# Summing the exponentials of a batch element's head pairs on GpSimd instead of TensorE

## Chip, cores and metric

One NeuronCore of a Trainium2 chip runs the whole program. The metric is the device time of one execution in microseconds (us); lower is better. TensorE multiplies matrices (PE in the profile; its weight loads are PEld), VectorE is DVE, ScalarE is ACT, GpSimd is POOL, and SyncE (SP) issues most transfers.

## What is computed

Attention with normalised queries and keys, then an MLP mixer on its output. Eight batch elements, 12 heads of 64, 448 positions; d_model is 768. Cut to what matters here:

```python
q_n, k_n = rmsnorm(q, g_q), rmsnorm(k, g_k)
scores = q_n @ k_n.T / 8
attn = exp(scores - max);  attn /= attn.sum(-1)      # the sum is what the change moves
x = (attn @ v)                                       # (B, S, 768)
h = relu(x.T @ w_tok1) @ w_tok2;  u = x + h.T        # token mixing
out = u + relu(u @ w_ch1) @ w_ch2                    # channel mixing
```

q, k and v are float32. The four weights arrive as 64-bit floats, and the kernel converts them itself.

## The kernel before

The work goes by head **pairs** p (two heads side by side on 128 partitions, six pairs in an element) and by **two pairs** t (pairs 2t and 2t+1). The first element therefore has t = 0, 1, 2. There are two arms, chosen at run time by the size of g_q and g_k; with these inputs the arm without a subtracted maximum runs (`shifted` is false).

For each t there are seven key blocks k of 64 keys. `score(t, k)` makes two PSUM tiles of scores (pool `ps_S`, four buffers) and ScalarE turns them into one SBUF tile `e` of 128x896 exponentials (pool `e_pool`, four buffers). `values(ps, k)` multiplies them by V into `o_ps`. The sums over keys, the denominators, are made in one of two ways, by `on_pe(p)`:

- on TensorE: `values` also calls `ones`, which multiplies every `e` by a block of ones and accumulates over the seven k in a PSUM tile of the pool `ps_M`;
- by additions: `group_sums(t, k)` adds the seven tiles `e` into one tile `es` (pool `es_pool`, one buffer), six additions of 128x896 for each t, and `row_sums(t)` then multiplies `es` alone by the ones, into two tiles `d_ps` of `ps_S`.

Before the change the first element (p below 6) uses the first way and all others the second, with the additions on VectorE. An `e` tile is free again when `values` has used it and, in the second way, `group_sums` as well (`used`).

`att_step(g)` lists one quarter of a t in program order: scores, transposes of later queries and keys (`turn_qk`), values, then the other engines' pieces. Every engine executes its own instructions in the order in which they are issued. The pieces that matter besides:

- `pre.roots(n, st)` forms 1/rms of pairs n and n+1: `guess` on VectorE (line 1473), then for n = 4 to 10 three Newton steps of four small GpSimd instructions each (lines 1481 to 1484); `scale` multiplies queries and keys by it on VectorE (line 1502), and `turn_qk` transposes them on TensorE (line 430). roots(4) stand at the end of t = 0, scale(4) and scale(5) at the start of t = 1, their transposes at its end; the same for 6 and 7 in t = 1 and t = 2.
- `denominators` turns the sums into reciprocals and multiplies the outputs, on VectorE (lines 558, 560, 572, 575); ScalarE first copies `o_ps` to `uT` (line 566).
- `trans_x(0, j)` transposes pair j's result (lines 816 and 818) for the token mixing `tok1` (line 840).
- `weight_items` converts the weights, spread over the same stage: five VectorE instructions for each chunk of 128x512 (lines 346, 347, 349, 351 and 380) and one on ScalarE between the last two (line 357). Up to t = 2 all chunks are merged with the attention's items in proportion to their costs by `merge`, so that a list with more cost in it shifts them a little.

Of the kernel before, what the change touches and what calls it, by code (L numbers as in the profile page):

```python
# [13 lines left out]
ALU = mybir.AluOpType  # L14
# [69 lines left out]
def whole(ctx, tc, shifted, pre, q, k, v, g_q, g_k, moe_w_tok1, moe_w_tok2, moe_w_ch1, moe_w_ch2, out):  # L84


    nc = tc.nc
# [10 lines left out]
    NPAIR = H // 2  # L98
# [53 lines left out]
    st = dict(pre.st)  # L152
# [339 lines left out]
    def group_sums(t, k):  # L492

        if k == 1:
            st["es", t] = es_pool.tile([P, 2, S], F32, name="es")
        es = st["es", t]
        nc.vector.tensor_tensor(out=es[:], in0=(es if k > 1 else st["e", t, 0])[:], in1=st["e", t, k][:], op=ALU.add)  # L497
        for i in (0, 1) if k == 1 else (k,):
            used(t, i)

    def on_pe(p):

        return shifted or p < NPAIR

    def ones(p, moving, **kw):

# [5 lines left out]
    def used(t, k):  # L512

        n = st["uses", t, k] = st.get(("uses", t, k), 0) + 1
        if n == 1 + (not on_pe(2 * t)):
            st.pop(("e", t, k))

    def values(ps, k):

        kw = dict(start=(k == 0), stop=(k == NK - 1))  # L520
        for p in ps:
            if k == 0:
                st["o", p] = ps_O.tile([P, 512], F32, name="o_ps")
                if on_pe(p):
                    st["d", p] = s_tile("d_ps") if shifted else m_tile()
            e, vt = exps(p, k), st["v", p]
            for a in range(2):
                rows = rows_of(p, a)
                nc.tensor.matmul(  # L529
                    out=st["o", p][a * D:(a + 1) * D, 0:S], lhsT=vt[rows, k * D:(k + 1) * D], rhs=e[rows, :], **kw)  # L530
        for p in ps:
            if on_pe(p):
                ones(p, exps(p, k), **kw)
        if not shifted:
            used(ps[0] // 2, k)
# [49 lines left out]
    def big_step(t, second):  # L585
# [31 lines left out]
        if not second:  # L617
            squares = [item(fn, i, st) for i in (n, n + 1) for fn in (pre.square, pre.reduce)] if more else []
            ahead, beside = (squares[:1], squares[3:]) if t > BIG else ([], [])
            between = [item(group_sums, t, k) for k in (1, 2) if live]  # L620
            ends, roots = ([(0.4, fn) for fn in fns] for fns in (denominators(last), pre.roots(n, st) if more else []))
            if t == BIG:
                return ahead, (5.4, first_block), beside, between + ends + [
                    item(load_v, i, c=0.0) for i in pair] + squares + roots
            between += roots[:1] + ends[:2] + roots[1:2]
            between += [it for both in zip(ends[2:], roots[2:4]) for it in both] if more else ends[2:]
            between += roots[4:] + [item(load_v, i, c=0.0) for i in pair if live]
            return ahead, (5.4, first_block), beside, between
        beside = [item(scale, n), item(scale, n + 1), item(turn_qk, n, 1), item(turn_qk, n, 0)] if more else []
        beside += [item(group_sums, t, k) for k in (3, 4)]  # L630
        between = [item(turn_qk, n + 1, 1), item(turn_qk, n + 1, 0)] + loads(n + 2) if more else []
        between += [item(group_sums, t, k) for k in (5, 6)] + loads(n + 3)
        return [], (6.2, second_block), beside, between

# [611 lines left out]
    for b in range(B):  # L1246
# [35 lines left out]
        elif b + AHEAD < B:  # L1282
            t = (b + AHEAD) * NPAIR // 2
# [290 lines left out]
```

## Time and profile before

| what | value |
|---|---|
| median of 3 executions | 1281.13 us (1280.3 to 1282.95) |
| the profiled execution | 1280.59 us |
| its span, first to last instruction | 1278.8 us |
| TensorE busy | 1249.1 us (98%) |
| VectorE busy | 796.8 us (62%) |
| ScalarE busy | 393.6 us (31%) |
| GpSimd busy | 394.8 us (31%) |
| granted TensorE clock | 0.997 |

The profiled execution is 0.5 us below the median, and 1.8 us of it lie outside the span. Busy shares are means over the whole span. The stage that the change touches lies between 20 and 90 us from the start, and the views below are of that stretch.

A row of the profile gives the line, the engine, the operation, what it writes and reads, the shape and how often; then busy time, and the idle time before it with what ended it. A row of the timeline starts with the start time and the duration in us. One float32 matmul of the program appears as two records.

### The profile page before, as it was taken

How to read it: one execution, taken by the hardware profiler on the slowest of the kernel's cores; microseconds unless marked ns; L12 is line 12 of the kernel's file. 1: busy time of each engine (PE TensorE's matmuls, PEld its weight loads, DVE VectorE, ACT ScalarE, POOL GpSimd, SP SyncE). 2: the span in 40 equal slices, each digit the busy share in tenths (PEclk: the TensorE clock that was granted, in tenths of full speed). 3: DMA queues.
4: the chain of work that ended last, by engine and by line, in shares of the span. 5: the costliest groups of instructions: out<-in, count | busy, mean ns of one | idle time of the engine just before them, and what ended most of it. 6: DMA issues, size and time to landing. Idle time of an engine off the chain costs nothing.

```text
span 1278.8 us, 20023 instructions
## 1 busy us (share of the span) xinstructions
PE 1249.1 (98%) x7236; PEld 887.4 (69%) x7236; DVE 796.8 (62%) x1241; ACT 393.6 (31%) x785; POOL 394.8 (31%) x637
## 2 busy tenths in 40 slices
PE   5999999999999899999999999999999999999998
PEld 2444444457745487796778768885887867797998
DVE  6999869756663355855668356765558456554233
ACT  6663433124330144402433044311343024300210
POOL 2302552043995611331223112241122322131222
PEclk9999999999999899999999999999999999999999
DMA  8767486999789876695657767585766865386554
GB/s 204 172 179 200 144 228 167 217 260 253 212 220 236 188 171 162 140 258 112 161 151 178 190 143 187 139 220 120 188 158 146 234 130 144 114 207 142 191 173 105
DMA packets 486784, 228.37 MB, mean 179 GB/s; under 512 B 368276, under 2 KB 446996, under 8 KB 486676
## 3 DMA queue, kind: packets, MB, share of 16 engines
q1 hardware_dynamic: 479682, 213.33, 67.5%
q0 software_dynamic: 3968, 12.98, 3.3%
q8 instruction: 59, 0.97, 0.3%
q10 hardware_dynamic: 3026, 0.69, 0.3%
q14 instruction: 49, 0.40, 0.1%
HBM read 184.26 MB, written 42.66 MB: 177 GB/s over the span
## 4 chain that ended last, share of the span: by engine, by line
PE 88%; DVE 5%; DMA 2%; SPq 1%; ACT 1%; issue 1%; DVEq 0%; ACTq 0%
PE m_ps L1002 25%; PE m_ps L1068 22%; PE s_ps L456 9%; PE o_ps L529 9%; PE m_ps L882 6%; PE m_ps L972 5%; PE m_ps L1051 4%; PE m_ps L840 2%; PE t_ps L840 2%; PE d_ps L509 1%; PE m_ps L509 1%; DVE es L497 1%; DVE raw L349 1%; DVE raw L347 1%; PE t_ps L430 1%
## 5 line engine op out<-in xcount | busy, mean ns | idle before, releaser
L1068 PE MATMUL m_ps<-hb,unit 128*128 128x224 f32 x1440 | 277.2, 354 | 0.0
L1068 PEld LDWEIGHTS m_ps<-hb,unit 128*128 128x128 f32 x1440 | 271.0, 190 | 8.9 <-issue 7.7
L1002 PE MATMUL m_ps<-tu,unit 128*128 128x224 f32 x1008 | 201.6, 355 | 1.3 <-ACT r L1012 1.3
L1002 PEld LDWEIGHTS m_ps<-tu,unit 128*128 128x128 f32 x1008 | 189.1, 190 | 15.0 <-issue 9.2
L460 ACT ACTIVATE e<-s_ps 128x448 f32<-128x448 f32 x294 | 138.7, 553 | 178.4 <-PE s_ps L456 169.8
L1002 PE MATMUL m_ps<-uT,unit 128*128 128x224 f32 x756 | 151.1, 354 | 0.0
L1002 PEld LDWEIGHTS m_ps<-uT,unit 128*128 128x128 f32 x756 | 142.2, 190 | 6.9 <-issue 3.9
L456 PE MATMUL s_ps<-qkT 64*64 64x448 f32 x1260 | 143.7, 545 | 0.8 <-ACT x L822 0.8
L529 PE MATMUL o_ps<-e,v 64*64 64x448 f32 x1148 | 129.4, 538 | 0.3 <-ACT uT L566 0.2
L497 DVE TENSOR_TENSOR es<-es,e 128x896 f32<-128x896 f32 x90 | 101.8, 1131 | 13.3 <-ACT e L460 8.6
L1008 DVE TENSOR_TENSOR hb<-m_ps,r 128x448 f32<-128x448 f32 x63 | 39.2, 622 | 108.8 <-POOL r L1008 56.7
L1008 POOL TENSOR_TENSOR hb<-r,r 128x448 f32<-128x448 f32 x21 | 23.8, 1132 | 246.0 <-ACT r L1024 246.0
L456 PEld LDWEIGHTS s_ps<-qkT 64*64 64x64 f32 x1260 | 44.9, 132 | 70.1 <-issue 60.6
L529 PEld LDWEIGHTS o_ps<-e,v 64*64 64x64 f32 x1148 | 45.1, 133 | 63.9 <-issue 60.4
L1481 POOL TENSOR_TENSOR nt<-rs 128x56 f32<-128x56 f32 (+1 forms) x54 | 22.4, 415 | 196.4 <-DVE rs L1473 193.6
L1009 ACT ACTIVATE hb<-hb 128x448 f32<-128x448 f32 x84 | 48.4, 577 | 99.4 <-DVE hb L1008 77.7
L321 POOL TENSOR_TENSOR raw<-raw 128x128 f32<-128x128 f32 x128 | 65.1, 528 | 34.6 <-DMA raw<-wp 30.1
L1083 POOL TENSOR_TENSOR uT<-uT,r 128x448 f32<-128x448 f32 x42 | 51.4, 1238 | 78.5 <-DVE r L1083 46.7
L882 PE MATMUL m_ps<-w_sb,h 128*128 128x448 f32 x192 | 75.2, 544 | 0.0
L1451 DVE TENSOR_REDUCE ms<-sq 128x28 f32<-128x896 f32 (+2 forms) x44 | 47.4, 1079 | 36.3 <-ACT sq L1438 28.2
L1008 DVE TENSOR_TENSOR r<-m_ps,r 128x448 f32<-128x448 f32 x42 | 26.1, 622 | 64.5 <-PE m_ps L1002 64.5
L887 DVE TENSOR_TENSOR uT<-uT,m_ps 128x448 f32<-128x448 f32 x48 | 29.4, 614 | 59.1 <-PE m_ps L882 59.0
(148 smaller groups left out, 1607.8 us busy)
## 6 DMA issues: line engine op xcount, KB each, us to landing
unit<-ws SPq DMA_DIRECT2D x267, 384.0 KB, 4.1
raw<-in_moe_w_ch_dram SPq DMA_DIRECT2D x72, 256.0 KB, 3.5
v<-in_v_dram SPq DMA_DIRECT2D x96, 112.0 KB, 4.1
out_dram<-turned SPq DMA_DIRECT2D x182, 56.0 KB, 1.9
xs<-xt SPq DMA_DIRECT2D x56, 168.0 KB, 4.6
qk_t<-in_q_dram SPq DMA_DIRECT2D x144, 56.0 KB, 3.6
qk_t<-in_k_dram SPq DMA_DIRECT2D x144, 56.0 KB, 3.7
x<-xs SPq DMA_DIRECT2D x42, 192.0 KB, 3.7
```

What stands on the lines that cost most here:

```text
L321: nc.gpsimd.tensor_tensor(out=at[o], in0=at[x], in1=at[y], op=ALU.add if op == "+" else ALU.subtract)
L456: nc.tensor.matmul(out=pss[i][rows_of(i, a), 0:S], lhsT=qkT[h, 1, k * D:(k + 1) * D], rhs=qkT[h, 0, :], start=True, stop=True)
L460: nc.scalar.activation(out=e[:, i, :], in_=pss[i][:, 0:S], func=AF.Exp)
L497: nc.vector.tensor_tensor(out=es[:], in0=(es if k > 1 else st["e", t, 0])[:], in1=st["e", t, k][:], op=ALU.add)
L529: nc.tensor.matmul(out=st["o", p][a * D:(a + 1) * D, 0:S], lhsT=vt[rows, k * D:(k + 1) * D], rhs=e[rows, :], **kw)
L840: nc.tensor.matmul(out=st["t1", h][jc][:, 0:HC], lhsT=w1_sb[:, c, jc * P:(jc + 1) * P], rhs=st["x", b, h][:, :, c, :], start=start and c = ...
L882: nc.tensor.matmul(out=ps[:, 0:S], lhsT=st["h1", jc][:, cc * P:(cc + 1) * P], rhs=w2_sb[:, jc].rearrange("p c r -> p (c r)"), start=(jc == ...
L972: nc.tensor.matmul(out=ps, lhsT=a[:, o + 2 * half, :], rhs=natural(half * KF + t) if wide else u[:, half * KC + t, :], start=(t == 0 and h ...
L1002: nc.tensor.matmul(out=ps[:, j * HS:(j + 1) * HS], lhsT=w[:, t, j, :], rhs=m, start=(t == 0), stop=(t == KC - 1))
L1008: add = lambda e, o, x, y: e.tensor_tensor(out=o, in0=x, in1=y, op=ALU.add)
L1068: nc.tensor.matmul(out=ps[:, x * HS:(x + 1) * HS], lhsT=st["w"][:, tile_at % 6, :], rhs=hb[:, X_SLOT[f], i, :], start=(i == 0), stop=(i == 3))
L1083: e.tensor_tensor(out=get(out), in0=get(x_), in1=get(y), op=ALU.add if op == "+" else ALU.subtract)
```

## The change

For pairs 2 to 5 (t = 1 and t = 2 of the first element) the denominators are made by `group_sums` and `row_sums` instead of `ones`, and these additions are given to GpSimd. Pairs 0 and 1 stay on TensorE, and all later elements keep VectorE.

```diff
         es = st["es", t]
-        nc.vector.tensor_tensor(out=es[:], in0=(es if k > 1 else st["e", t, 0])[:], in1=st["e", t, k][:], op=ALU.add)
+        e = nc.gpsimd if 2 * t < NPAIR else nc.vector
+        e.tensor_tensor(out=es[:], in0=(es if k > 1 else st["e", t, 0])[:], in1=st["e", t, k][:], op=ALU.add)
         for i in (0, 1) if k == 1 else (k,):
             used(t, i)
 
     def on_pe(p):
 
-        return shifted or p < NPAIR
+        return shifted or p < 2
```

Through `on_pe`, three other places follow: `values` no longer calls `ones` for these pairs, `used` waits for two users of an `e` tile instead of one, and `att_step` adds the six `group_sums` items (cost 0.5 each in `merge`) and one `row_sums` for each t. The added line moves every later line number by one.

## The prediction

> **What bounds the kernel now.** I read the page first (TensorE busy 98% of the span), then the busy time by stretches over the stage concerned:
>
> ```profile
> 20.00:40.00 20.00, 19.93 (x198) 8.35 (x192) 18.08 (x34) 13.67 (x27) 2.87 (x5) 1.00 1.11 231
> 40.00:60.00 20.00, 19.76 (x186) 9.07 (x184) 19.31 (x34) 13.99 (x29) 4.74 (x12) 1.00 0.51 144
> 60.00:80.00 20.00, 19.27 (x180) 8.82 (x176) 18.91 (x34) 12.39 (x27) 4.27 (x8) 1.00 0.71 205
> ```
>
> The columns after the length are PE, PEld, DVE, ACT, POOL. TensorE sets the pace, but VectorE has only 0.7 to 1.9 us of 20 free; GpSimd is nearly empty. So TensorE time is worth something here only while VectorE keeps up. TensorE's timeline prices the removed matmuls:
>
> ```profile
> 53.05 0.93 PE L509 MATMUL m_ps<-e,one_c 64*64 64x448 f32 x8
> 53.80 0.93 PE L529 MATMUL o_ps<-e,v 64*64 64x448 f32 x8
> 54.56 0.93 PE L509 MATMUL m_ps<-e,one_c 64*64 64x448 f32 x8
> ```
>
> Start to start, one key block of ones for two pairs takes 0.75 us, as much as its values. Last, the timelines of VectorE, GpSimd and TensorE show who feeds whom between t = 1 and t = 2:
>
> ```profile
> 56.62 0.18 DVE L1473 TENSOR_SCALAR rs<-ms 112x32 int32<-112x32 int32 x1
> 56.88 0.95 POOL L1481 TENSOR_TENSOR nt<-rs 112x32 f32<-112x32 f32 x1 [14.39 <-DVE rs L1473]
> 67.20 2.35 DVE L1502 TENSOR_TENSOR qk_t<-qk_t,rs 112x1024 f32<-112x1024 f32 x2
> 70.34 1.91 PE L430 MATMUL t_ps<-ident,qk_t 112*128 112x112 f32 x16 [0.26 <-ACT e L460]
> ```
>
> VectorE's guess for pairs 6 and 7 starts GpSimd's twelve Newton steps (to 64.84), these release VectorE's scale (ends 69.55), and TensorE's transposes start 0.8 us later. The chain VectorE-GpSimd-VectorE-TensorE has under 1 us of slack, and the added work stands on its two middle engines.
>
> **What the skill says.** The Trainium skill, "SBUF — State Buffer", Who interferes with whom: VectorE and GpSimd share a pair of SBUF ports under an exclusive lock; a VectorE instruction with two SBUF inputs, or in a two-port mode, blocks and is blocked by a GpSimd instruction that reads SBUF. The trace agrees, to the instruction:
>
> ```profile
> 214.71 2.78 POOL L984 TENSOR_TENSOR uT<-uT,r 128x448 f32<-128x448 f32 x2 [18.00 <-ACT r L983]
> ...
> 214.51 0.69 DVE L349 SCALAR_TENSOR_TENSOR raw<-raw 128x512 uint32<-128x512 uint32 x1
> 215.24 1.25 DVE L351 TENSOR_SCALAR raw<-raw 128x512 uint32<-128x512 uint32 x1
> 216.41 3.15 DVE L497 TENSOR_TENSOR es<-es,e 128x896 f32<-128x896 f32 x2
> ```
>
> Line 351 takes 0.43 us elsewhere and 1.25 here; the first of the two line 497 additions takes 2.02 instead of 1.09. They alternate: one VectorE instruction, one of GpSimd. "GPSIMD Engine Reference", Elementwise: GpSimd needs 1.96 times VectorE's time for a float32 addition. The exact shape stands in the trace, at 1.92 times:
>
> ```profile
> L1042 DVE TENSOR_TENSOR hb<-hb x42: 1026/1082/2026, 494.0 to 1244.7; 128x896 f32<-128x896 f32 x42
> L1042 POOL TENSOR_TENSOR hb<-hb x18: 2074/2082/2092, 491.8 to 1254.9; 128x896 f32<-128x896 f32 x18
> ```
>
> **The change part by part.**
>
> Removed from TensorE: 7 blocks of ones for each t, 14 x 0.75 = 10.5 us; added: `row_sums` twice, 2 x 0.75 = 1.5. Net -9.0 us of TensorE work: the most that can be gained.
>
> Added to GpSimd: 12 x 2.08 = 25.0 us. In its queue six additions of t = 1 stand after Newton(4), then Newton(6), then the six of t = 2. With the lock, a blocked VectorE instruction loses about 1.93 of each 2.08 us (at 216.41 line 497 lost 0.93 behind the last 0.99 us of a GpSimd addition; start-up overlaps). Contended are lines 346, 347, 349, 351, 380, 497, 575, 1502; transposes, reductions and reciprocals run beside GpSimd (at 511 us line 558 keeps its 0.59).
>
> *t = 1.* ScalarE's exponential of k = 1 ends at 42.4 (41.47 plus two of 0.5), and Newton(4) by 42.5, so the first addition starts at 42.4. Each takes 2.08 plus about 0.5 waiting for VectorE's current instruction: 42.4 + 6 x 2.57 = 57.8. TensorE without its ones would reach `row_sums(1)` at 57.67 - 5.25 = 52.4; it waits until 57.8, adds 0.85 with the handover, and starts the next transposes at 58.7 instead of 57.67: **+1.0 us**, the gain of t = 1 gone. Behind that wait nothing else is lost. The earlier wait for scale(5), about 51 instead of 48.8, lies inside it.
>
> *VectorE's lag.* Six blocks of 1.93 are 11.6 us, 0.6 of it under one transpose: 11.0. The guess at 56.62 moves to about 68.0 (0.4 for handovers). Newton(6), 8.0 us before (56.88 to 64.84), takes 7.5: 68.2 to 75.7. Only then do the additions of t = 2 start.
>
> *t = 2.* By 76.2 VectorE has redone the work up to line 347 of the chunk before the scales. Left are lines 349 (0.55 after a release), 351 (0.3), a transpose (covered), 575 (0.5) and two 1502 (1.1 each), each preceded by one addition of 2.0: the scales end at 76.2 + 5 x 2.0 + 3.5 = 89.7, the sixth addition at 91.7. The transposes, held in TensorE's queue with all values and scores behind them, end at 90.7 instead of 72.2: +18.5. Four blocks without ones win back 3.0, `row_sums(2)` costs 0.75: the transposes at 79.11 come at 95.4, **+16.3**.
>
> *The end of the stage.* VectorE, free at 91.7, needs the 15.6 us of work that stood between 69.55 and 86.45 (16.9 less 1.3 idle): the last outputs are scaled at 107.3 instead of 86.45. TensorE wants them for its transposes at 88.98 and now gets there at 107.3: **+18.3 us**. This is the sum: 28 us of waiting less 9 us of work. From 100 to 140 us TensorE is busy all the time, so nothing makes this up; VectorE, 83% busy from 120 on, catches up in the background.
>
> At nothing I cost: the chunk order (the guess of pairs 4 and 5 moves 2.6 us ahead, hidden by GpSimd's idle time); one transfer of a chunk moved past others on SP's queue (a chunk is converted well before its matmuls: first at 53.8, used at 117.9); GpSimd's own transfers, whose first is at 102.7, behind Newton(8). What the trace doesn't show: `d_ps` now takes two of the four `ps_S` buffers until line 558 reads them, and VectorE is late (about 72), so TensorE's scores of t = 2 stop there, and four `e` tiles wait for additions. Both waits lie before 89.7 and are covered; their bounds are 0 and 5 us (0 taken; a gain is excluded, since a buffer held longer starts nothing earlier). The lock's loss is bounded by 0 and 2.08 for each addition; I take 1.93.
>
> **Rivals.**
> *Faster: the additions are hidden.* If VectorE lost nothing, they would end at 42.4 + 12.5 = 54.9, and the next transposes start at 55.8 (-1.9); the guess and Newton(6) unmoved (64.84), those of t = 2 end at 77.3 and TensorE is at 78.2 instead of 79.11. The last outputs at 86.45 allow at most -2.5: about 1279, down to 1272 (all 9.0) if VectorE's work slipped behind. It decides by VectorE's total loss: under about 2.5 us, 0.2 for each addition, it gains. For it: GpSimd's idle columns. Against: the 2.02 us row, eight times that loss.
> *Slower by half.* VectorE mostly gets the ports first and loses about half, 11 us: last outputs at 97.5 instead of 86.45, against 88.98: +8.5, 1289.6. For it: Newton's first step at 36.75 waited through two VectorE instructions. Against: line 351 above lost at once.
> *Slower by more.* The buffer waits add their 5, and VectorE's lag of 21 holds later scales too, 2 to 3: about 1307.
> *It doesn't do what it says*: excluded: in the changed program's instruction order 12 additions stand on GpSimd, and TensorE has 56 matmuls with ones less and 8 more.
>
> **How the numbers follow.** The profiled execution, 1280.59 (span 1278.8 and 1.8 around it), is 0.5 below the median; 1280.6 + 18.3 + 0.5 = 1299.4. Chances: forecast 0.50, half 0.20, more 0.15, hidden 0.15, of which 0.10 gains over 0.2% (2.6 us, about what a measurement can tell from no change) and 0.05 lies within it. The range reaches from just below half (1286) to above more (1310).
>
> **What would show it.** Right: 12 GpSimd rows of 2.1 to 2.8 us at line 498; conversion lines up to 2.5 us in the stage; idle TensorE of 20 us or more between 58 and 92, ended by line 1503 or by `es`; the last scaled outputs near 107. Wrong: conversion rows unchanged, or the first `tok1` at or before 80.67.

## The result and the profile after

The changed kernel takes **1300.32 us** (median of 4, 1298.84 to 1303.05) against 1281.35 (1280.3 to 1282.95) for the kernel before beside it: ratio 1.0152, 95% interval 1.0133 to 1.0172, or 19.0 us more. The prediction said 1299.4. The profiled execution is the longest of the four: 1303.05 us, span 1300.4. All line numbers of the changed kernel are one higher (the additions are L498, the guess L1474, the scale L1503).

Busy time by stretches of the kernel after (length, then PE, PEld, DVE, ACT, POOL, the granted clock, DMA share, GB/s), for the stage shown of before and the 40 us behind it:

```profile
20.00:40.00 20.00, 20.00 (x202) 9.30 (x194) 17.48 (x35) 13.49 (x27) 4.94 (x12) 1.00 1.08 231
40.00:60.00 20.00, 15.18 (x117) 7.31 (x119) 19.62 (x16) 11.39 (x23) 15.97 (x6) 0.83 0.18 54
60.00:80.00 20.00, 12.45 (x90) 4.63 (x84) 19.45 (x28) 10.28 (x22) 10.94 (x15) 0.74 0.60 168
80.00:100.00 20.00, 12.76 (x80) 6.30 (x73) 19.52 (x23) 8.42 (x18) 9.69 (x4) 0.74 0.33 98
100.00:120.00 20.00, 17.42 (x93) 7.45 (x92) 19.24 (x32) 11.36 (x27) 5.35 (x9) 0.91 0.73 188
```

Up to 40 us little has changed (Newton's steps for pairs 4 and 5 start at 33.35 instead of 36.75). From 40 to 60 VectorE is as busy as before (19.62 and 19.31), but with 16 instructions instead of 34: on average one takes twice as long. TensorE falls to 12 to 15 us of 20. Busy time says nothing here of work done; the counts in brackets do.

GpSimd's timeline of the kernel after (start, duration, row; in brackets the idle time before and what ended it):

```profile
42.42 2.11 POOL L498 TENSOR_TENSOR es<-e 128x896 f32<-128x896 f32 x1 [3.22 <-ACT e L460]
44.61 14.18 POOL L498 TENSOR_TENSOR es<-es,e 128x896 f32<-128x896 f32 x5
67.89 0.95 POOL L1482 TENSOR_TENSOR nt<-rs 112x32 f32<-112x32 f32 x1 [9.10 <-DVE rs L1474]
73.72 2.39 POOL L498 TENSOR_TENSOR es<-e 128x896 f32<-128x896 f32 x1
76.19 7.12 POOL L498 TENSOR_TENSOR es<-es,e 128x896 f32<-128x896 f32 x3
85.39 6.53 POOL L498 TENSOR_TENSOR es<-es,e 128x896 f32<-128x896 f32 x2 [2.08 <-ACT e L460]
```

Six additions from 42.42 to 58.79, Newton's steps for pairs 6 and 7, and six from 73.72 to 91.92. VectorE's timeline of the kernel after, over the second six and to the stage's end:

```profile
74.08 2.32 DVE L346 TENSOR_SCALAR cv_sb<-raw 128x512 uint32<-128x512 uint32 x1
76.44 2.46 DVE L347 SCALAR_TENSOR_TENSOR raw<-raw,cv_sb 128x512 f32<-128x512 uint32 x1
78.94 2.45 DVE L349 SCALAR_TENSOR_TENSOR raw<-raw 128x512 uint32<-128x512 uint32 x1
81.42 2.18 DVE L351 TENSOR_SCALAR raw<-raw 128x512 uint32<-128x512 uint32 x1
...
84.26 0.62 DVE L576 TENSOR_TENSOR uT<-uT,rd 128x448 f32<-128x448 f32 x1
84.80 4.24 DVE L1503 TENSOR_TENSOR qk_t<-qk_t,rs 112x1024 f32<-112x1024 f32 x2
...
105.73 0.63 DVE L576 TENSOR_TENSOR uT<-uT,rd 128x448 f32<-128x448 f32 x1
```

In the kernel before, two of these conversion lines and the last outputs read:

```profile
70.53 0.69 DVE L347 SCALAR_TENSOR_TENSOR raw<-raw,cv_sb 128x512 f32<-128x512 uint32 x1
71.99 0.43 DVE L351 TENSOR_SCALAR raw<-raw 128x512 uint32<-128x512 uint32 x1
...
85.83 0.62 DVE L575 TENSOR_TENSOR uT<-uT,rd 128x448 f32<-128x448 f32 x1
```

After, each line from 346 to 351 takes 2.2 to 2.5 us where it took 0.42 to 0.70: it has waited through one addition. Between 83.3 and 85.39 GpSimd had no `e` to add (the 2.08 in its timeline), and in just that gap line 576, which reads two SBUF operands as well, keeps its 0.62. The excess of the blocked VectorE instructions over their usual durations adds up to 21.3 us for the 12 additions, 1.77 each; each addition held up one VectorE instruction. The last outputs, at 85.83 before, now start at 105.73: 19.9 later. From 38 us until they end at 106.36 VectorE's timeline shows no wait at all (before, it waited 1.3 us in this stage), so nothing that TensorE or ScalarE did can have delayed them: VectorE's own longer instructions did.

TensorE's timeline of the kernel after, where it waits or runs long:

```profile
64.99 0.90 PE L817 MATMUL t_ps<-ident,uT 128*128 128x128 f32 x3 [4.08 <-ACT e L460]
71.27 3.18 PE L456 MATMUL s_ps<-qkT 64*64 64x448 f32 x12 [3.47 <-DVE dt L559]
...
86.12 1.73 PE L430 MATMUL t_ps<-ident,qk_t 112*128 112x112 f32 x8 [5.37 <-ACT e L460]
89.14 1.73 PE L430 MATMUL t_ps<-ident,qk_t 112*128 112x112 f32 x8 [1.30 <-ACT qkT L436]
90.80 5.15 PE L530 MATMUL o_ps<-e,v 64*64 64x448 f32 x32
...
107.48 0.49 PE L817 MATMUL t_ps<-ident,uT 128*128 128x128 f32 x3
```

The waits of 5.37 and 1.30 us are put down to ScalarE, but what these transposes read are the scales of line 1503: the second half starts at 89.14, 0.1 us after VectorE has finished them (84.80 and 4.24). The last transposes of the stage start at 107.48; before, they started at 88.98:

```profile
88.98 0.49 PE L816 MATMUL t_ps<-ident,uT 128*128 128x128 f32 x3
```

**18.5 us later**: that is nearly all of the loss.

### The profile page after: what moved, and what is told of

The parts are those of the page before. It is cut to its first block, busy times and chain, and to the rows that moved or that the text cites. A ratio compares the mean times of both kernels' runs of the same rounds, so it can differ in the third digit from the quotient of the medians.

```text
span 1300.4 us, 19849 instructions
## 1 busy us (share of the span) xinstructions
PE 1253.3 (96%) x7140; PEld 890.7 (68%) x7140; DVE 817.5 (63%) x1241; ACT 394.8 (30%) x785; POOL 425.7 (33%) x649
## 4 chain that ended last, share of the span: by engine, by line
PE 86%; DVE 8%; DMA 2%; ACT 2%; issue 1%; SPq 1%; DVEq 0%; ACTq 0%
PE m_ps L1003 25%; PE m_ps L1069 21%; PE s_ps L456 9%; PE o_ps L530 9%; PE m_ps L883 5%; PE m_ps L973 5%; PE m_ps L1052 4%; PE m_ps L841 2%; PE t_ps L841 2%; DVE raw L347 1%; DVE raw L349 1%; PE d_ps L510 1%; DVE ms L1452 1%; PE t_ps L430 1%; DVE cv_sb L346 1%
## 5 line engine op out<-in xcount | busy, mean ns | idle before, releaser
L456 PE MATMUL s_ps<-qkT 64*64 64x448 f32 x1260 | 148.1, 553 | 5.7 <-DVE dt L559 3.5
L498 DVE TENSOR_TENSOR es<-es,e 128x896 f32<-128x896 f32 x90 | 103.3, 1148 | 12.3 <-ACT e L460 7.6
L530 PEld LDWEIGHTS o_ps<-e,v 64*64 64x64 f32 x1148 | 47.3, 137 | 66.6 <-issue 63.5
L1482 POOL TENSOR_TENSOR nt<-rs 128x56 f32<-128x56 f32 (+1 forms) x54 | 21.3, 395 | 181.3 <-DVE rs L1474 178.5
```

Of the source, the lines that this page charges most:

```text
L456: nc.tensor.matmul(out=pss[i][rows_of(i, a), 0:S], lhsT=qkT[h, 1, k * D:(k + 1) * D], rhs=qkT[h, 0, :], start=True, stop=True)
L498: e.tensor_tensor(out=es[:], in0=(es if k > 1 else st["e", t, 0])[:], in1=st["e", t, k][:], op=ALU.add)
L530: nc.tensor.matmul(out=st["o", p][a * D:(a + 1) * D, 0:S], lhsT=vt[rows, k * D:(k + 1) * D], rhs=e[rows, :], **kw)
```

## The experiments

The prediction's theory: GpSimd's additions hold the read port that VectorE needs for its second SBUF input, and VectorE, which has no idle time in this stage, falls behind by nearly every microsecond of them. The rivals: the loss comes from GpSimd's own queue (Newton's steps behind six additions); from `row_sums` waiting for sums that come late; from `d_ps` in the buffers of the scores; or from TensorE's clock, since it idles.

### The same GpSimd time without its SBUF reads

Each addition of the first element is replaced by a copy of two elements for each partition, which keeps its waits, and two fills of the whole tile: about the same time on GpSimd, with hardly any reading. The sums over key blocks are left out.

```diff
-        e.tensor_tensor(out=es[:], in0=..., in1=st["e", t, k][:], op=ALU.add)
+        if 2 * t < NPAIR:
+            e.tensor_copy(out=es[:, 0, 0:2], in_=st["e", t, k][:, 0, 0:2])
+            for i in range(2):
+                e.memset(es[:], 400.0)
+        else:
+            ...
```

> Each of the twelve GpSimd additions becomes a copy of two columns of e (it still waits for the exponential) and two memsets of es, about as long as the addition (some 2.3 us) but hardly reading SBUF; the sums of pairs 2 to 5 are left out. Ports theory (VectorE loses 1.93 us behind each addition because both read SBUF): most VectorE instructions go free, only the two-port ones (lines 346 and 351) may still be blocked; the scales of pairs 6 and 7 end near 70 to 76 us instead of 89, and the time is 1279 to 1288 us. Rivals: if the length of GpSimd's queue is what holds TensorE (row_sums and Newton behind the additions), or the two d_ps tiles in ps_S, or the lowered TensorE clock by itself, it stays near 1300.

Measured: 1280.49 us against 1281.4, ratio 0.9999 (0.9989 to 1.001). GpSimd's timeline of this kernel:

```profile
47.22 1.75 POOL L501 MEMSET es<- 128x896 f32 x2
49.03 0.26 POOL L499 COPY es<-e 128x2 f32<-128x2 f32 x1
```

and VectorE's, beside the first of these fills:

```profile
47.15 0.69 DVE L347 SCALAR_TENSOR_TENSOR raw<-raw,cv_sb 128x512 f32<-128x512 uint32 x1
47.88 0.69 DVE L349 SCALAR_TENSOR_TENSOR raw<-raw 128x512 uint32<-128x512 uint32 x1
48.61 0.65 DVE L351 TENSOR_SCALAR raw<-raw 128x512 uint32<-128x512 uint32 x1
```

From 40 to 100 us GpSimd is busy 35.8 us here and 36.6 in the changed kernel; what stands in its queue behind each addition, the order of all engines and the buffers are the same. Lines 347 and 349 keep their 0.69 us in the middle of GpSimd's work; line 351 takes 0.65 instead of 0.43 here (1.19 at most). VectorE's whole excess is 2.3 us, and the loss is gone. What costs the 19 us is that GpSimd reads SBUF, not that it is busy or that something stands behind it in its queue. Whether an instruction that reads one SBUF operand instead of two would cost as much was not tried.

The queue is not free. In this trace TensorE waits 2.43 and 2.38 us at `row_sums` for GpSimd's fills, then runs at half clock, and its last transposes come 2.2 us later than before (88.98), although VectorE's outputs are in time:

```profile
91.14 0.49 PE L822 MATMUL t_ps<-ident,uT 128*128 128x128 f32 x3
```

The traced execution took 1284.0 us, 3.5 above the median of this kernel. So these rivals are worth some 2 us there, and in the median nothing that can be measured.

### Shorter additions

The additions take 448 of 896 columns, or 16; `es` is filled on GpSimd beforehand. The rest of the sum is left out. (`first` is the tile `e` of block 0 for k = 1, and `es` after that.)

```diff
+                nc.gpsimd.memset(st["es", t][:], 400.0)
...
+            e.tensor_tensor(out=es[:, 0, 0:448], in0=first[:, 0, 0:448],
+                            in1=st["e", t, k][:, 0, 0:448], op=ALU.add)
```

> Each addition covers 128x448 instead of 128x896 (half of the sums of pairs 2 to 5 are left out; the rest of es is filled once by a memset). Ports theory: the blocked part falls from 1.93 to about 0.98 us, VectorE's lag at the end of the stage from 20 to about 11 us, and the time is 1288 to 1292 (+8.5 by the same sum as in the prediction). Buffers or clock alone: no reason for half, near 1300 or near 1281.

> The same with 128x16 (nearly all of the sums left out): twelve additions of some 0.2 us in the same places of GpSimd's queue, the same waits, buffers and order, and TensorE without its ones. Ports theory: VectorE loses under 1 us in all, and the change gains what VectorE's position allows: 1278.5 to 1281. Buffers theory (d_ps in ps_S, e tiles with two users): still slower than before by several us. If TensorE alone bounded the stage: 1272.

Measured: with 448 columns 1287.28 us, ratio 1.0041 (1.0022 to 1.0061); with 16 columns 1281.14, ratio 1.0002 (0.9989 to 1.0015); both beside 1281.4. In one table:

| additions on GpSimd | VectorE's excess | last outputs start (before: 85.83) | TensorE's last transposes start (before: 88.98) | time against before |
|---|---|---|---|---|
| 128x16 | 0.35 us | 85.56 | 87.84 | -0.3 us |
| none, but fills | 2.3 us | 86.22 | 91.14 | -0.9 us |
| 128x448 | 8.9 us | 94.10 | 95.78 | +5.9 us |
| 128x896 (the change) | 21.3 us | 105.73 | 107.48 | +19.0 us |

Time follows VectorE's excess, with about 2 to 3 us of it absorbed. The half-length additions cost less than half: 0.74 us for each of 12, where I had put 0.98, and 1287.3 us lies just under the 1288 to 1292 expected.

The 16-column kernel is the test of the rival "hidden", too: nothing is lost on VectorE and TensorE has 9.0 us less to do, yet no gain can be measured (1281.14, just above the 1278.5 to 1281 expected). In its trace TensorE is 1.1 us ahead at the last transposes. Then it waits for a copy by ScalarE:

```profile
91.27 2.89 PE L456 MATMUL s_ps<-qkT 64*64 64x448 f32 x10 [1.93 <-ACT x L829]
```

The wait was 0.84 us before. ScalarE is late because it had stood 3.06 us for a load of keys (0.90 before), and after the wait TensorE runs 3.4 us at half clock. At 116.82 its next `row_sums` are 1.4 us behind the kernel before (115.47). VectorE's last outputs do not take the gain away here: they end at 86.19, and TensorE comes to them at 86.97, straight from other work. It had waited 4.72 us before, at 61.72, for VectorE to empty `d_ps`; that wait is taken up below. How the 9.0 us divide between these waits and the slow clock is not shown.

### The additions alone, with TensorE's ones kept

The denominators come from TensorE as before the change; GpSimd makes the twelve additions all the same, and nobody uses their sums.

```diff
...
-        return shifted or p < 2
+        return shifted or p < NPAIR
...
-        if n == 1 + (not on_pe(2 * t)):
+        if n == 1 + (t > 0):
...
-        if live and not on_pe(p):
+        if live and t and not shifted:
```

> The kernel before, with its ones on TensorE for all six pairs, and the twelve GpSimd additions beside it, whose result nobody uses. Ports theory: VectorE is delayed as in the changed kernel and still sets the end of the stage: 1297 to 1302. If the wait of row_sums, the d_ps tiles in ps_S or a clock lowered by an idle TensorE were the cause, it is near 1281 to 1285, since none of the first two is there and TensorE has 10.5 us more to do.

Measured: 1303.4 us, ratio 1.0171 (1.0154 to 1.0188): 22.0 us more than before, 3 more than the change, and just above the 1297 to 1302 expected. VectorE's timeline of this kernel:

```profile
84.96 4.24 DVE L1505 TENSOR_TENSOR qk_t<-qk_t,rs 112x1024 f32<-112x1024 f32 x2
...
105.87 0.63 DVE L578 TENSOR_TENSOR uT<-uT,rd 128x448 f32<-128x448 f32 x1
```

The scales and last outputs come within 0.2 us of where the changed kernel has them, though no `row_sums` waits for a sum and no `d_ps` takes a score's buffer. Neither of these rivals is needed for the loss. TensorE keeps its 10.5 us of ones here and loses little by it, since it was waiting anyway: its last transposes start at 108.85, 1.4 after the changed kernel's. TensorE still waits and still runs at half clock in this trace, so this kernel does not test the clock; what speaks against the clock is VectorE's timeline above, which has no wait in it.

### The additions on VectorE

```diff
-        e = nc.gpsimd if 2 * t < NPAIR else nc.vector
+        e = nc.vector
```

> The additions of pairs 2 to 5 on VectorE instead of GpSimd, nothing else changed. Ports theory: VectorE gets 12 x 1.09 = 13.1 us more work but is never blocked; its last outputs of the stage come at 86.45 + 13.1 = 99.5 instead of 86.45, against 88.98 where TensorE wants them: +10.6, 1290 to 1293 us. So GpSimd, with its own 25 us idle before, costs VectorE more than doing the work itself. If only the added dependence on additions or the buffers mattered, it would be near 1300.

Measured: 1291.7 us against 1280.22, ratio 1.0096 (1.0061 to 1.0131): 11.5 more, for 10.6 expected. Twelve additions of 1.09 us are 13.1 us on VectorE, and the last outputs start at 97.88, 12.0 later. So the additions cost VectorE less if it makes them itself than if GpSimd makes them for it: 13.1 us against 21.3.

### Another pool for the denominators

```diff
-            st["d", p] = s_tile("d_ps")
+            st["d", p] = m_tile() if p < NPAIR else s_tile("d_ps")
```

> The changed kernel with row_sums of pairs 2 to 5 in the pool ps_M, as the ones were before, instead of ps_S. Prediction: the wait for line 559 (3.5 us at 71 in the changed kernel) is covered by the later wait for the scales; same time within 2 us, 1298 to 1302. If the d_ps tiles in ps_S are part of the cause, 3 to 5 us less.

> As e4_tiny (128x16 additions, nearly all of the sums left out), with row_sums of pairs 2 to 5 in ps_M. Theory: what kept e4 from gaining was TensorE's 4.7 us at the scores for VectorE's line 565 (d_ps in ps_S); without it TensorE runs ahead until VectorE's last outputs at 85.4 bind: 2 to 3 us faster than before, 1278 to 1279.5. If VectorE or the clock alone holds it: same as before, within 1 us.

Measured: on the changed kernel 1299.58 us, ratio 1.0148 (1.0108 to 1.0187), the last outputs at 106.18: no difference. On the 16-column kernel 1279.21 us, ratio 0.9995 (0.9982 to 1.0007) beside 1280.78: inside the range expected, but no difference that can be measured; the 2 to 3 us hoped for did not show. The wait of 3.47 us at 71.27 for line 559 is real and covered.

### One half of the change at a time

Additions for t = 1 only, and for t = 2 only; the other two pairs keep TensorE's ones.

```diff
-        return shifted or p < 2
+        return shifted or p // 2 in (0, 2)    # t = 1 only
+        return shifted or p < 4               # t = 2 only
```

> Only pairs 2 and 3 on GpSimd, pairs 4 and 5 with ones on TensorE. Ports theory: VectorE lags 11 us from 58 on, the guess of pairs 6 and 7 is at 67.6 as in the changed kernel, but no additions follow: scales at 81, last outputs near 97.5 against 88.98: +8.5, about 1290.

> Only pairs 4 and 5 on GpSimd. Ports theory: nothing lags until Newton(6) ends near 64.8; then six additions block VectorE for 11 us: scales near 78, last outputs near 97.5: +8.5, about 1290. The two halves should add up to about the whole less the 2.5 us of slack that each alone finds: 8.5 + 8.5 + 2.5 = 19.5.

Measured: t = 2 alone 1289.7 us, ratio 1.0075 (1.0055 to 1.0095), 9.5 more for 8.5 expected. Part of that agreement is luck: the last outputs start at 93.87, where the sum had them near 97.5, and the traced execution, 1287.73 us, is the second fastest of seven. **t = 1 alone missed**: 1296.57 us, ratio 1.0128 (1.0095 to 1.0162), 16.4 more for 8.5 expected. The halves do not add: 16.4 + 9.5 is 25.9, not 19.0. ScalarE's timeline with t = 1 only:

```profile
55.47 0.76 ACT L357 ACTIVATE raw<-raw,expo_c 128x512 uint32<-128x512 uint32 x1 [7.46 <-DVE raw L351]
```

TensorE's:

```profile
56.70 3.25 PE L430 MATMUL t_ps<-ident,hb 112*128 112x112 f32 x16 [7.67 <-ACT e L460]
...
73.81 3.25 PE L456 MATMUL s_ps<-qkT 64*64 64x448 f32 x12 [6.53 <-DVE dt L559]
```

and VectorE's:

```profile
94.72 0.65 DVE L559 STREAM_TRANSPOSE dt<-m_ps 128x448 f32<-128x448 f32 x1 [6.51 <-PE m_ps L510]
```

ScalarE stood 7.46 us at a weight conversion whose line 351 came late from VectorE, where three conversion lines in a row had been blocked; the exponentials behind it were late, TensorE waited 7.67 for them, and then 6.53 for VectorE to empty `d_ps`. With its ones of t = 2 still to do, TensorE became the late one: at 94.72 VectorE waits for it. I moved `d_ps` away from the scores in this kernel too:

> As e7_t1_only (pairs 2 and 3 on GpSimd, 1296.6), with their row_sums in the pool ps_M instead of ps_S. In e7 TensorE waited 6.5 us at its scores for VectorE's line 559 to free d_ps, and in the end VectorE waited 6.5 us for TensorE. If that buffer is what e7 lost above its forecast, the wait goes and the time is the 8.5 above before that VectorE's lag alone gives, 1288 to 1291. If e7's excess was the half clock (20 us of it), it stays near 1296.

Measured: 1293.85 us against 1280.78, ratio 1.0114 (1.0089 to 1.0138), 13.1 more. That is neither of the two values expected. By the medians 2.7 us have gone, and the two intervals overlap, so even that is not certain; more than half of what was missing stays. ScalarE's wait remains in that trace, and VectorE still waits 3.87 us for TensorE. TensorE's time at half clock falls with the wait, from 20.5 to 10.2 us, so the runs do not separate the buffers from the clock. How the 16.4 divides between ScalarE's queue, the buffers and the clock stays open.

## Why the prediction was right, step by step

- **The bound and the mechanism hold.** VectorE's blocked time sets the stage. The table of doses, the fills and the unused additions show it from three sides, and in the changed kernel VectorE has no wait left from 38 to 106.36. What the Trainium skill states in "SBUF — State Buffer", Who interferes with whom, agrees: two SBUF inputs on VectorE meet a GpSimd instruction that reads SBUF and wait, and they do not meet one that only writes (0.69 us beside a fill, 2.46 beside an addition). That the thing held is a port is the page's statement; the runs show that it is GpSimd's reading that matters.
- **1.93 us lost for each addition** was a little too much: 1.77, or 21.3 us in all instead of 23.2.
- **"The chain has under 1 us of slack"** holds for its last link alone. Newton's steps were done at 64.84 and the scale started at 67.20, 2.4 us later, behind VectorE's own queue; after the change 73.61 and 84.80. The sum is not touched by it, because it follows VectorE's queue.
- **t = 1: the next transposes at 58.7** failed. They start at 64.99. `row_sums(1)` comes at 59.99, 2.2 behind the forecast (the values before it ran at half clock, to 59.4), and then TensorE waits 4.08 for an exponential. ScalarE's timeline of the changed kernel gives the reason:

```profile
59.83 0.78 ACT L357 ACTIVATE raw<-raw,expo_c 128x512 uint32<-128x512 uint32 x1 [3.85 <-DVE raw L351]
63.76 0.76 ACT L357 ACTIVATE raw<-raw,expo_c 128x512 uint32<-128x512 uint32 x1 [3.15 <-DVE raw L351]
64.42 0.95 ACT L460 ACTIVATE e<-s_ps 128x448 f32<-128x448 f32 x2
```

  ScalarE's exponential stands in order behind two conversions that wait for VectorE. "Behind that wait nothing else is lost" overlooked this queue. The queue reaches TensorE through the buffers: `d_ps` holds two of the four of `ps_S`, and the transposes need one that this exponential frees. With `row_sums` in the other pool the same transposes start at 61.26, right after the row sums. The miss is covered, since TensorE waits for the scales of t = 2 anyway; in the kernel with t = 1 alone the same queue comes to the front.
- **The guess at 68.0** came at 67.63. **Newton(6) in 7.5 us** took 5.7 (67.89 to 73.61), so the additions of t = 2 began 2.0 us before their time; the 2.08 us that GpSimd waited for an `e`, again ScalarE's, gave that back: they end at 91.92, forecast 91.7.
- **Scales at 89.7, transposes at 90.7**: 89.04 and 90.87.
- **The transposes of results at 95.4** came at 97.41: the four blocks of values took 5.15 us instead of 3.0, most of them at half clock, which was not foreseen.
- **The last outputs at 107.3** ended at 106.36, and **TensorE's +18.3** is +18.5 at 107.48. Two small errors cancel: the outputs come 0.9 us early, and the last transposes start 1.1 us after them, behind two others, which the sum left out. TensorE waited 0.32 us before these three, so it arrives with VectorE, and the lost clock cost next to nothing on top.
- **"28 us of waiting less 9 us of work"** is 27.3 by its own terms, and in the trace it divides otherwise. From 40 us to its last transposes TensorE idles 19.9 us where it idled 1.6: 18.3 more. It is busy 47.6 us where it was busy 47.3, with 9.0 us of matmuls gone: running slowly took back what they had freed. The end is the same, since TensorE waits for VectorE either way.
- **Nothing makes it up later** holds, but a little is added in the profiled execution: by 116.5 us matching instructions are 20.9 late. TensorE waited 2.26 us at 111.24 for a copy by ScalarE, which had stood 3.96 for a load of queries and keys, and ran at half clock until 115.2. For the profiled execution the sum gave 1298.9 and it took 1303.05; the median, 1300.32, is 0.9 above the forecast. The close agreement owes something to errors of opposite sign, and to that extent it is luck.
- **The signs named.** The conversion lines (up to 2.46 us) and the last outputs came as named. TensorE's idle time between 58 and 92 is 14.2 us, not 20 or more, since it runs slowly as well; and three of the 12 additions take 2.9 to 3.9 us, over the 2.8 named.
- **The rivals.** "Half" fell with 1.77 lost of 2.08. "Hidden" named its condition rightly, a loss on VectorE under 2.5 us, but the gain it promised did not show: the three kernels with fills or 16 columns measure the same as before. The evidence quoted against it is misreckoned: the 2.02 us row loses 0.93, under five times the 0.2 allowed, not eight. "More" is not needed: the buffer wait is covered. **The costs put at nothing** (the chunk order, the moved transfers) are too small to measure: the kernel with fills has all of them, and its median is that of the kernel before. It also has 9.0 us less to do on TensorE, so a few microseconds could hide there. The guess of pairs 4 and 5 moved 3.4 us, not 2.6.

## What to carry to other kernels

Before giving an elementwise operation with two SBUF inputs to an idle GpSimd, look at what VectorE runs beside it: where those rows read two SBUF operands or run in a two-port mode and VectorE has no idle time, price the move at nearly GpSimd's whole duration on VectorE's path (1.77 of 2.08 us here), which is more than VectorE would need to do it (1.09). Fills of about the same length, which read next to nothing, cost nothing that could be measured. Work taken from the busiest engine was worth nothing in this stage, where it waits for pieces that other engines deliver: ask first whose piece it waits for last. And follow each blocked engine through the queues of the others: an engine that merely waits for it, ScalarE here, may hold something urgent behind that wait.

## What the hardware did that I had not expected

TensorE that waits can be slow afterwards. The changed kernel's trace has half the full clock at 50.3 us (for 6.8), 64.0 (10.2), 84.5 (10.2) and 111.8 (3.4); the kernel before has no such stretch in this stage. The Trainium skill, "TensorE: Matmul & The Clock Gate", Part 1, describes a clock that falls to half after an idle window of about 3.4 us, and the lengths seen are multiples of that. The waits do not fit it as well: those at the four stretches are 3.04, 4.08, 5.37 and 2.26 us long, two of them shorter than the window, and in the 448-column kernel a wait of 2.27 us (to 99.55) has no slow stretch after it. So the length of a wait alone did not tell whether the clock would fall.

In t = 2 the slow clock cost 2.1 us on the four blocks of values and 1.6 on the transposes of queries and keys (1.73 us for each eight records, where all sixteen took 1.91 before), nearly all of it beside VectorE's lag.
